# Attention and gated MLP on one core: keys times values of four head pairs as one section, half the keys loaded into U's space, weight sums written to V's space, new orders

## Chip, core and metric

The kernel runs on one core of a Trainium2 chip. The metric is the time of one execution on the device in microseconds (us); less is better. Five engines take part, each with its own instruction queue: TensorE (PE, with its weight loads as PEld), VectorE (DVE), ScalarE (ACT), GpSimd (POOL) and SyncE (SP). In this kernel POOL and SP do little but issue DMAs.

## What is computed

The inputs q, k, v have 8 batches, 8 heads, 576 positions and 64 channels. A linear attention with RMS norm gives x, and a gated MLP with a spatial product follows:

```python
kv = np.einsum('bhsd,bhse->bhde', k, v)
out = np.einsum('bhsd,bhde->bhse', q, kv)
rms = np.sqrt(np.mean(out * out, axis=-1, keepdims=True) + 1e-06)
x = (out / rms * g_norm)          # heads side by side: 8 x 576 x 512
h = np.maximum(x @ w_in, 0.0)     # 512 x 1024
u, v = h[..., :512], h[..., 512:]
v_n = (v - mean(v)) / np.sqrt(var(v) + 1e-06)
v_s = np.einsum('ts,bsd->btd', w_spatial, v_n) + b_spatial[None, :, None]
out = (u * v_s) @ w_out           # 512 x 512
```

All data are float32; w_in and w_out come as 64-bit numbers that the kernel decodes itself.

## The kernel before

**Products.** A large matmul is split: each float32 operand becomes a high and a low part of the type fp32r (`split`, or XH/XL, VH/VL, GH/GL), and three products high*high, high*low, low*high go to one bank (`three`, `hv_k`, `multiply`). For u and for the spatial product, batches 1 to 7 and 2 to 7 use a scheme with seven block products in place of eight (`u_steps`, `sp_steps`; their orders are the tables SEVEN and GATED). It needs sums of blocks: `x_sums` adds blocks of x (batch by batch), `w_sums` adds blocks of w_in once, in batch 1, and writes the sums to a DRAM buffer `spare_u`, from which each batch's `to_u` loads them into UX (L878).

**Attention.** A batch has four pairs of heads. `att_k` takes keys times values of some pairs in float32 on 64x64 quarters of the array (L162, bank `pskv`), the copies L179 and L180 put the result in KVB (even batches) or KVO0/KVO1 (odd ones), `att_q` multiplies it with the queries (L234, bank `pso`) and normalises (L217 to L226), `att_t` transposes (L262, bank `pstr`), and L255/L256 split x into XH and XL. Each batch of 1 to 7 has two sections of two pairs, a section being the matmuls of one call of `att_k`. SP loads keys and values (L142, 512 KB a pair, into the two buffers KV0 and KV1; a remainder of 64 rows into KT0 and KT1 at L143) and queries (L152). A load is issued by `issue`, when fewer than two pairs lie in wait, and waits for the section that last read its buffer.

**MLP.** `hv` forms v (L345, bank `psh`; ReLU L318, norm L324 to L332, split L348/L349), the u steps fill U, the spatial products (banks psa, psb, psc) end in a tail product from TA and TB (L559, L561), `gate` multiplies with U (L573, L575) and splits into G, and `out_unit` multiplies G with w_out (L312, bank `pso2`), copies the bank on ACT to a tile `o` (L655) and stores it (L657). The four banks of the pool ps_mm serve psh, the u products, the spatial products and pso2 in turn. The tile `o` has two buffers of the tag "stg", and so have the tiles `w` into which `w_sums` puts its parts before POOL writes them out (L475): the same two buffers.

**Order.** Batch 0 with all weights' decoding is a prologue set by the table PLAN (letters for steps; W is a weight load, L an attention load). Batch 1 follows FIRST, even batches EVEN, odd ones ODD: v, u, p, o are units of the MLP, s is the next attention step of a later batch, w one half of `w_sums`. The framework's scheduler may move instructions between these marks.

The lines that are needed:

Of the kernel before, what the change touches and what calls it, by code (L numbers as in the profile page):

```python
# [8 lines left out]
F32 = mybir.dt.float32  # L9
# [8 lines left out]
DM, FF = 512, 1024  # L18
# [28 lines left out]
p10 p11 p60 p21 p20 p61 p50 p70 p51 p71 p41 p30 p40 p31  # L47
# [3 lines left out]
p10 p11 p60 p50 p70 p20 p40 p61 p51 p21 p30 p71 p41 p31  # L51
# [3 lines left out]
p p p p s p p p p p p s p p p p o s w s s s o o o s s s s w o s s  # L55
# [3 lines left out]
v s s s v v v u s y s s s s u u u u u s u u u u u s u u u s s s s p p p p p s p s s s p s s p p p p  # L59
s p s s p p o o o o s s s  # L60
# [3 lines left out]
v v v u v u u u u u u s u u s u u u u u s s p p s p p p s p p p s p s p p p s s p p s o s o o s s s  # L64
o s o
# [8 lines left out]
def body(ctx: ExitStack, tc, qT, kvm, kvt, g2, w_in, wsT, bsp, w_out, out):  # L74
# [43 lines left out]
    KVB = persistent([P, 2, P], F32, "KVB")  # L118
    KVO = [persistent([P, 2, P], F32, f"KVO{i}") for i in range(2)]
# [3 lines left out]
    KT = [persistent([P, 2, P], F32, f"KT{i}") for i in range(2)]  # L123
# [12 lines left out]

    def att_load(b, p, kind):
        if kind in "fek":
            kv, kt = (x[n_load[0] % 2] for x in (KV, KT))
            n_load[0] += 1  # L140
            for i, j in ((0, 2), (2, NC)) if (b, p) == (0, 0) else ((0, NC),):
                nc.sync.dma_start(kv[:, :, i:j], kvm[b, p, :, :, i:j])  # L142
            nc.sync.dma_start(kt[0:TAIL], kvt[b, p])  # L143
            keys[b, p] = kv, kt, None
        if kind == "k":
            qs = load.tile([P, P], F32, name="qs", tag="qs")
            nc.sync.dma_start(qs, qT[b, p, :, S - P:S])
            keys[b, p] = kv, kt, qs
        if kind in "fq":
            n = NT if b % 2 else S  # L150
            qt = load.tile([P, S], F32, name="qt", tag="qt")
            nc.sync.dma_start(qt[:, 0:n], qT[b, p, :, 0:n])  # L152
            queries[b, p] = qt

    def att_k(b, pairs, st, copy=nc.vector.tensor_copy):
        ps = ps_att.tile([P, 512], F32, name="pskv", tag="att")
        to = KVO[pairs[0] // 2] if b % 2 else KVB
        ends, first = [], None

        def product(p, of, h, c):  # L160
            at = (p - pairs[0]) * P + h
            return nc.tensor.matmul(ps[h:h + D, at:at + D], of[:, 0, h:h + D], of[:, 1, h:h + D],  # L162
                                    start=c == 0, stop=c == NC)

        for p in reversed(pairs):
            kv, kt, qs = keys.pop((b, p))
            for c in range(NC + 1):
                of = kv[:, :, c] if c < NC else kt
                for h in (0, D):
# [5 lines left out]
            st[p] = to[:, p % 2]  # L175
            ends.append((p, qs))
        both = ps[:, 0:len(pairs) * P].rearrange("p (j e) -> p j e", e=P)
        own = slice(p % 2, p % 2 + len(pairs))
# [107 lines left out]
    def att_steps(b):  # L286
# [12 lines left out]
        K = [lambda p=p: att_k(b, (p, p + 1), st) for p in (0, 2)]  # L299
# [3 lines left out]
        if b % 2 == 0:  # L303
            return [K[0], Q[0], Q[1], T[0], K[1], Q[2], T[1], Q[3], t2, T[3], end], []
# [156 lines left out]
    def w_sums(kk):  # L461
# [315 lines left out]
    for b in range(1, B):  # L777
# [4 lines left out]
        todo += [(b, p, kind) for kind, ps in kinds for p in ps]  # L782
    states = {}
    wanted = [0]

    def issue():

        while wanted[0] and todo and (len(queries) if todo[0][2] == "q" else len(keys)) < 2:
            wanted[0] -= 1
            att_load(*todo.pop(0))  # L790
# [4 lines left out]

    nc.vector.memset(KVB[:, 1], 0.0)
    nc.vector.memset(epsc, EPS)
# [4 lines left out]
    for kvb in KVO:  # L802
        nc.gpsimd.memset(kvb, 0.0)
# [120 lines left out]
    def first():  # L924
# [4 lines left out]
        for d in range(4):  # L929
            if d == 2:  # L930
                enqueue(2)
                enqueue(3)
# [9 lines left out]
    def batch(b):  # L942
# [6 lines left out]
        if b % 2 and b > 1:  # L949
            enqueue(b + 1)  # L950
            enqueue(b + 2)
        for token in (FIRST if b == 1 else ODD if b % 2 else EVEN).split():
# [8 lines left out]
            elif token == "p":  # L961
                p.pop(0)()
            elif token == "o":
# [62 lines left out]
```

## Time and profile before

| | us |
|---|---|
| runs | 507.4, 507.61, 505.15 (median 507.4) |
| profiled execution | 505.66, span 503.9 |
| busy share of PE, DVE, ACT, POOL | 97%, 76%, 58%, 7% |

The profile follows one execution; its span, from the first to the last recorded event, is 1.8 us under that execution's time. A busy share is an average over stages, so the waits of PE (the queries on waits and the timeline) tell more than the shares do.

### The profile page before, as it was taken

How to read it: one execution, taken by the hardware profiler on the slowest of the kernel's cores; microseconds unless marked ns; L12 is line 12 of the kernel's file. 1: busy time of each engine (PE TensorE's matmuls, PEld its weight loads, DVE VectorE, ACT ScalarE, POOL GpSimd, SP SyncE). 2: the span in 40 equal slices, each digit the busy share in tenths (PEclk: the TensorE clock that was granted, in tenths of full speed). 3: DMA queues.
4: the chain of work that ended last, by engine and by line, in shares of the span. 5: the costliest groups of instructions: out<-in, count | busy, mean ns of one | idle time of the engine just before them, and what ended most of it. 6: DMA issues, size and time to landing. Idle time of an engine off the chain costs nothing.

```text
span 503.9 us, 9784 instructions
## 1 busy us (share of the span) xinstructions
PE 487.6 (97%) x3520; PEld 441.4 (88%) x3520; DVE 380.5 (76%) x1016; ACT 291.0 (58%) x1013; POOL 35.6 (7%) x70
## 2 busy tenths in 40 slices
PE   7699999999998999999999999999999999999996
PEld 6579999998987899889998899989998899978995
DVE  1597978866967697967985789868788579986870
ACT  3789854956415894468433686457732587446421
POOL 5000110000002210010000000010000101010000
PEclk8999999999999999999999999999999999999999
DMA  7998352453164648361274426343461514124213
GB/s 233 320 327 265 103 160 74 157 189 126 48 184 132 188 128 291 120 211 42 80 250 131 146 59 231 119 156 119 147 220 44 187 44 153 46 52 157 100 70 105
DMA packets 28917, 74.51 MB, mean 148 GB/s; under 512 B 3810, under 2 KB 8418, under 8 KB 27332
## 3 DMA queue, kind: packets, MB, share of 16 engines
q1 hardware_dynamic: 23412, 48.01, 29.8%
q0 software_dynamic: 5456, 25.87, 15.5%
q8 instruction: 28, 0.46, 0.4%
q14 instruction: 21, 0.17, 0.1%
HBM read 58.48 MB, written 13.11 MB: 142 GB/s over the span
## 4 chain that ended last, share of the span: by engine, by line
PE 56%; issue 19%; ACT 11%; DVE 7%; DMA 4%; POOL 1%; SPq 1%; POOLq 0%; ACTq 0%; DVEq 0%
PE pso L312 13%; PE psh L345 9%; PE psb L553 5%; PE psc L553 4%; PE psa L553 3%; PE psub L553 3%; PE pso L234 3%; ACT x L217 2%; PE psuc L553 2%; PE psua L553 2%; PE pskv L162 2%; PE psu L553 2%; PE pstr L262 2%; PE psh L312 2%; DMA stage<-w_in 1%
## 5 line engine op out<-in xcount | busy, mean ns | idle before, releaser
L312 PE MATMUL pso<-WO,G 128*128 128x512 f32 x384 | 94.1, 396 | 0.0
L312 PEld LDWEIGHTS pso<-WO,G 128*128 128x128 f32 x384 | 70.7, 188 | 14.8 <-ACT o L655 0.4
L348 ACT CAST G<-SUMg 128x288 fp32r<-128x288 f32 (+1 forms) x56 | 22.9, 408 | 51.5 <-DVE SUMg L575 51.0
L217 ACT ACTIVATE x<-pso 128x64 f32<-128x64 f32 x216 | 46.2, 254 | 9.1 <-PE pso L234 9.0
L345 PE MATMUL psh<-WVH,XH 128*128 128x512 f32 x112 | 44.3, 395 | 1.6 <-ACT o L655 1.6
L655 ACT COPY o<-pso 128x512 f32<-128x512 f32 x35 | 19.9, 591 | 44.0 <-PE pso L312 35.4
L217 ACT ACTIVATION_READ_ACCUMULATOR x<-pso 128x1 f32 x216 | 45.2, 238 | 0.0
L345 PE MATMUL psh<-WVH,XL 128*128 128x512 f32 x112 | 43.9, 392 | 0.0
L345 PE MATMUL psh<-WVL,XH 128*128 128x512 f32 x112 | 43.7, 390 | 0.0
L349 DVE TENSOR_TENSOR VL<-v,VH 128x512 fp32r<-128x512 f32 (+1 forms) x56 | 34.4, 621 | 8.5 <-ACT VH L348 8.0
L348 ACT CAST VH<-v 128x512 fp32r<-128x512 f32 (+1 forms) x56 | 31.3, 570 | 5.4 <-DVE v L377 4.1
L349 DVE TENSOR_TENSOR G<-SUMg,G 128x288 fp32r<-128x288 f32 (+1 forms) x56 | 23.4, 419 | 6.0 <-ACT G L348 5.7
L324 DVE BATCH_NORM_STATS2 s<-v 128x6 f32<-128x512 f32 x32 | 22.0, 689 | 7.3 <-ACT v L318 7.1
L345 PEld LDWEIGHTS psh<-WVH,XH 128*128 128x128 f32 x112 | 21.0, 188 | 6.5 <-ACT o L655 2.5
L255 ACT ACTIVATE XH<-pstr,gcol 128x512 fp32r<-128x512 f32 x28 | 19.5, 699 | 12.0 <-PE pstr L262 10.0
L332 ACT ACTIVATE v<-v,mv,rv 128x512 f32<-128x512 f32 x28 | 23.0, 823 | 5.5 <-DVE mv L331 5.5
L553 PE MATMUL psb<-WSH,VH 128*128 128x288 f32 x84 | 25.9, 309 | 0.0
L345 PEld LDWEIGHTS psh<-WVH,XL 128*128 128x128 f32 x112 | 21.0, 188 | 4.4
L553 PE MATMUL psb<-WSL,VH 128*128 128x288 f32 x84 | 24.7, 295 | 0.0
L345 PEld LDWEIGHTS psh<-WVL,XH 128*128 128x128 f32 x112 | 21.0, 188 | 4.2
L553 PE MATMUL psb<-WSH,VL 128*128 128x288 f32 x84 | 24.5, 294 | 0.0
L234 PE MATMUL pso<-KVB,qt 128*128 128x128 f32 x128 | 19.6, 287 | 3.5 <-ACT KVB L180 2.3
(245 smaller groups left out, 1429.0 us busy)
## 6 DMA issues: line engine op xcount, KB each, us to landing
KV<-kvm SPq DMA_DIRECT2D x31, 512.0 KB, 4.9
WO<-spare_o POOLq DMA_DIRECT2D x12, 1024.0 KB, 6.5
UX<-spare_u POOLq DMA_DIRECT2D x18, 512.0 KB, 5.7
out<-o SPq DMA_DIRECT2D x32, 256.0 KB, 2.3
qt<-qT SPq DMA_DIRECT2D x16, 288.0 KB, 4.5
stage<-w_in SPq DMA_DIRECT2D x8, 512.0 KB, 7.0
qt<-qT SPq DMA_DIRECT2D x16, 256.0 KB, 3.2
KT<-kvt SPq DMA_DIRECT2D x32, 64.0 KB, 4.7
```

The costliest lines, as they stand in the source:

```text
L162: return nc.tensor.matmul(ps[h:h + D, at:at + D], of[:, 0, h:h + D], of[:, 1, h:h + D], start=c == 0, stop=c == NC)
L217: nc.scalar.activation(x[:, cols], ps[0:rows, cols], AF.Square, accum_out=ss[:, h:h + 1])
L234: nc.tensor.matmul(ps[:, c * P:(c + 1) * P], qt[:, c * P:(c + 1) * P], st[p], start=True, stop=True)
L255: nc.scalar.activation(hi, ps, AF.Copy, scale=gcol)
L312: nc.tensor.matmul(ps, lt, rh, start=i == 0, stop=i == n - 1)
L324: nc.vector.bn_stats(s6, v)
L332: nc.scalar.activation(v, v, AF.Identity, bias=m, scale=r)
L345: nc.tensor.matmul(ps, lt, rh, start=k == 0 and i == 0, stop=k == NP - 1 and i == 2)
L348: nc.scalar.copy(hi, x)
L349: nc.vector.tensor_tensor(lo, x, f32(hi), op=ALU.subtract)
L553: nc.tensor.matmul(ps, lt, rh, start=start and i == 0, stop=stop and i == len(pairs) - 1, skip_group_check=True)
L655: nc.scalar.copy(o, ps)
```

## The change

Keys times values of batches 3 to 7 become one section of four pairs, the token k; the result goes to one KVB for four pairs, and KVO0 and KVO1 go. Of these batches (and of batch 0) pairs 2 and 3 are loaded into the space of U, which is free between a batch's last gate and the next batch's first u step; the token l issues these loads, two batches ahead of their batch. KT has four tiles. Batch 0's pairs 2 and 3 lie in U, too, with their queries in SUMp1 and SUMu2, so that none of its loads waits for a buffer. The parts in `w_sums` are written to VH and VL in place of the `stg` tiles. All order tables are new.

```diff
+[ W G | L N8 c C J00 D00 L W B00 J01 L c W L A01 n6 C X0 T00 B01 J02 c W W A02 T01 H00 J03 W B02 C
...
-v v v u v u u u u u u s u u s u u u u u s s p p s p p p s p p p s p s p p p s s p p s o s o o s s s
-o s o
+v v v v k u u u u u u u u u u u s u u u s u s p p p s p s p p p p p p p p p s p s o l o o s s o o
...
-    KVB = persistent([P, 2, P], F32, "KVB")
-    KVO = [persistent([P, 2, P], F32, f"KVO{i}") for i in range(2)]
+    KVB = persistent([P, NP, P], F32, "KVB")
...
+    KVU = [flat_u[:, i * n_kv:(i + 1) * n_kv].rearrange("p (j c e) -> p j c e", c=NC, e=P) for i in range(2)]
+    QSU = [flat_u[:, 2 * n_kv + i * P:2 * n_kv + (i + 1) * P] for i in range(2)]
+    def in_u(b, p):
+        return p > 1 and b not in (1, 2)
...
+            if in_u(b, p):
+                kv, kt = KVU[p - 2], KT[p]
+            else:
+                kv, kt = KV[n_load[0] % 2], KT[n_load[0] % 2]
+                n_load[0] += 1
...
+            if kind == "f" and p > 1:
+                qt = SUM[("p1", "u2")[p - 2]].rearrange("p j t -> p (j t)")
...
-        K = [lambda p=p: att_k(b, (p, p + 1), st) for p in (0, 2)]
+        K = [] if b > 2 else [lambda p=p: att_k(b, (p, p + 1), st) for p in (0, 2)]
...
-            parts = [work.tile([P, DM], F32R, name="w", tag="stg", bufs=2) for _ in range(2)]
-            parts = [w.rearrange("p (n f) -> p n f", f=HF)[:, 0:n.stop - n.start] for w in parts]
+            parts = [w[:, kk, n] for w in (VH, VL)]
...
+            elif token == "k":
+                if b + 1 < NB:
+                    att_k(b + 1, range(NP), states.setdefault(b + 1, {}))
+                if b % 2 == 0:
+                    enqueue(b + 1)
+            elif token == "l":
+                if b + 2 < NB:
+                    for p in (2, 3):
+                        att_load(b + 2, p, "k" if b % 2 else "e")
```

The lines move by 9 to 15: L162 becomes L174, L180 L192, L345 L357, L312 L324, L553 L564, L561 L572, L575 L586, L655 L666, L475 L486. PE has the same matmuls in both kernels.

**SP at the start of the program**, before. The names are the loads' targets: gcol the norm's factors, KV and KT keys and values of a pair, qt its queries, stage a block of w_in.

```order
L907 DMA gcol_109<-g2 128x1
L142 DMA KV0_104<-kvm 128x2x256 x2
L143 DMA KT0_106<-kvt 64x256
L152 DMA qt_152<-qT 128x576
L675 DMA stage_176<-w_in 128x1024
L142 DMA KV1_105<-kvm 128x1024
L143 DMA KT1_107<-kvt 64x256
L152 DMA qt_205<-qT 128x576
L142 DMA KV0_104<-kvm 128x1024
```

And now:

```order
L686 DMA stage_149<-w_in 128x1024
L922 DMA gcol_109<-g2 128x1
L151 DMA KV0_102<-kvm 128x2x256 x2
L152 DMA KT0_104<-kvt 64x256
L164 DMA qt_155<-qT 128x576
L151 DMA KV1_103<-kvm 128x1024
L152 DMA KT1_105<-kvt 64x256
L164 DMA qt_206<-qT 128x576
L686 DMA stage_208<-w_in 128x1024
L151 DMA U_100<-kvm 128x1024
L152 DMA KT2_106<-kvt 64x256
```

The first block of w_in goes ahead of all; the second one goes ahead of the third pair's keys, which now go to U.

**PE between batches 2 and 3.** Before, batch 4's first section lies among batch 2's spatial products, and its second one directly behind the last tail product (psc); the output products (pso2) follow:

```order
L553 MATMUL psc_2523<-WSH_84,VL_95 128x288
L559 MATMUL psc_2523<-WTH_86,TA0_96 128x288
L561 MATMUL psc_2523<-WTL0_87,TB0_98 128x288
L262 MATMUL pstr_2999<-ident_108,x_2917 128x128 x4
L162 MATMUL pskv_3022<-KV1_105 64x64 x8
L162 MATMUL pskv_3022<-KT1_107 64x64 x2
L162 MATMUL pskv_3022<-KV0_104 64x64 x8
L162 MATMUL pskv_3022<-KT0_106 64x64 x2
L312 MATMUL pso2_2596<-WO_2313,G_2312 128x512 x8
L312 MATMUL pso2_2612<-WO_2313,G_2312 128x512 x3
```

Now one section of four pairs of batch 4 stands behind batch 2's last output products and ahead of the first product of batch 3 (psh); between the last tail product and the section lie 39 products of pso2, of which these are the last 14:

```order
L324 MATMUL pso2_2618<-WO_2299,G_2298 128x512 x7
L324 MATMUL pso2_2634<-WO_2299,G_2298 128x512 x7
L174 MATMUL pskv_2803<-U_100 64x64 x8
L174 MATMUL pskv_2803<-KT3_107 64x64 x2
L174 MATMUL pskv_2803<-U_100 64x64 x8
L174 MATMUL pskv_2803<-KT2_106 64x64 x2
L174 MATMUL pskv_2803<-KV1_103 64x64 x8
L174 MATMUL pskv_2803<-KT1_105 64x64 x2
L174 MATMUL pskv_2803<-KV0_102 64x64 x8
L174 MATMUL pskv_2803<-KT0_104 64x64 x2
L357 MATMUL psh_2671<-WVH_76,XH_89 128x512
L357 MATMUL psh_2671<-WVL_77,XH_89 128x512
```

The section has pairs 3 and 2 (from U) first. The same place it has at the other boundaries from batch 1 to batch 6; from 1 to 2, 12 output products follow it, and from 3 to 4 and 5 to 6, 43 products lie ahead of it.

**POOL at the sums of w_in.** Before, the parts leave from w tiles, and the last one stands behind the first load of UX:

```order
L475 DMA spare_u_82<-w_1838 128x256
L475 DMA spare_u_82<-w_1839 128x256
L475 DMA spare_u_82<-w_1844 128x2x256
L475 DMA spare_u_82<-w_1845 128x2x256
L475 DMA spare_u_82<-w_1990 128x256
L475 DMA spare_u_82<-w_1991 128x256
L475 DMA spare_u_82<-w_1996 128x2x256
L878 DMA UX_2019<-spare_u_82 128x1024
L475 DMA spare_u_82<-w_1997 128x2x256
L878 DMA UX_2019<-spare_u_82 128x1024 x2
```

Now they leave from VH and VL:

```order
L486 DMA spare_u_82<-VH_94 128x256
L486 DMA spare_u_82<-VL_95 128x256
L486 DMA spare_u_82<-VH_94 128x256
L486 DMA spare_u_82<-VL_95 128x256
L486 DMA spare_u_82<-VH_94 128x2x256 x2
L486 DMA spare_u_82<-VL_95 128x2x256 x2
L893 DMA UX_1939<-spare_u_82 128x1024 x3
L410 DMA TB0_98<-TA0_96 64x768
L410 DMA TB1_99<-TA1_97 64x768
```

All eight DMAs to spare_u stand ahead of the loads of UX (a row with x2 is two).

## Rows read from the trace of the kernel before

**Rows 1.** Part 1 of the page: busy time by engine

```profile
PE 487.6 (97%) x3520; PEld 441.4 (88%) x3520; DVE 380.5 (76%) x1016; ACT 291.0 (58%) x1013; POOL 35.6 (7%) x70
```

**Rows 2.** PE's waits: line, awaited operation, us in total, times, longest

```profile
PE pstr L262 <- DVE x L226: 2.3, 1, 2.3
PE pso L234 <- ACT KVB L180: 2.3, 3, 1.2
PE psh L345 <- ACT o L655: 1.6, 2, 1.4
...
PE psua L553 <- ACT U L506: 0.7, 1, 0.7
```

**Rows 3.** Timeline of PE around a section: start, us, instruction, count

```profile
250.55 0.29 PE L553 MATMUL psb<-WSH,VL 128*128 128x288 f32 x1
250.77 0.69 PE L162 MATMUL pskv<-KV 128*64 128x64 f32 x16
...
252.09 0.40 PE L553 MATMUL psc<-WSH,VL 128*128 128x288 f32 x1
252.33 0.30 PE L559 MATMUL psc<-WTH,TA 128*128 128x288 f32 x1
252.46 0.30 PE L561 MATMUL psc<-WTL,TB 128*128 128x288 f32 x1
```

**Rows 4.** Timeline of PE from batch 1 to 2; in brackets the wait

```profile
152.74 2.00 PE L312 MATMUL pso<-WO,G 128*128 128x512 f32 x8
156.14 0.50 PE L345 MATMUL psh<-WVH,XH 128*128 128x512 f32 x1 [1.40 <-ACT o L655]
156.47 0.39 PE L345 MATMUL psh<-WVL,XH 128*128 128x512 f32 x1
156.70 0.40 PE L345 MATMUL psh<-WVH,XL 128*128 128x512 f32 x1
```

**Rows 5.** Timeline of ACT there

```profile
155.52 0.57 ACT L655 COPY o<-pso 128x512 f32<-128x512 f32 x1
```

**Rows 6.** Timeline of DVE there

```profile
151.18 0.43 DVE L349 TENSOR_TENSOR w<-v,w 128x256 fp32r<-128x256 f32 x1 [4.21 <-DMA out<-o]
```

**Rows 7.** Timeline of POOL, 160 to 176 us: UX's loads

```profile
167.26 0.57 POOL L878 DMA_DIRECT2D UX<-spare_u  x1 [0.95 <-DMA spare_u<-w]
...
173.60 1.12 POOL L878 DMA_DIRECT2D UX<-spare_u  x2 [5.05 <-DMA spare_u<-w]
```

**Rows 8.** Timeline of PE: last tail products of batches 2 and 5

```profile
205.59 0.29 PE L561 MATMUL psc<-WTL,TB 128*128 128x288 f32 x1
...
380.93 0.30 PE L561 MATMUL psc<-WTL,TB 128*128 128x288 f32 x1
```

**Rows 9.** Timeline of DVE: last gates of batches 2 and 5

```profile
210.13 0.46 DVE L575 SCALAR_TENSOR_TENSOR SUMg<-U,SUMg 128x288 f32<-128x288 f32 x1
...
381.75 0.46 DVE L575 SCALAR_TENSOR_TENSOR SUMg<-U,SUMg 128x288 f32<-128x288 f32 x1
```

**Rows 10.** Timeline of SP: two pairs' loads

```profile
206.98 0.33 SPq L142 DMA_DIRECT2D KV<-kvm  x1
...
207.96 0.54 SPq L142 DMA_DIRECT2D KV<-kvm  x1
```

**Rows 11.** Instructions of L142, 194 to 214 us, their landing

```profile
DMA to landing us min/median/max: 3.6/4.3/4.9
```

**Rows 12.** Timeline of PE in the prologue

```profile
8.03 2.05 PE L234 MATMUL pso<-KVB,qt 128*128 128x128 f32 x8 [1.25 <-DMA qt<-qT]
...
15.17 0.63 PE L262 MATMUL pstr<-ident,x 128*128 128x128 f32 x4 [2.29 <-DVE x L226]
```

**Rows 13.** Timeline of ACT in the prologue

```profile
10.14 0.66 ACT L700 ACTIVATE t<-stage 128x512 f32<-128x512 f32 x1 [2.83 <-DMA stage<-w_in]
...
11.55 0.22 ACT L217 ACTIVATE x<-pso 128x64 f32<-128x64 f32 x1
```

**Rows 14.** Windows: stretch, busy by engine, PE's granted clock, DMA share, GB/s

```profile
8.00:12.00 4.00, 3.97 (x22) 3.96 (x22) 0.87 (x2) 1.80 (x7) 0.00 (x0) 0.62 1.01 358
```

More of the change, by code (lines that the diff above doesn't have):

```diff
@@ L117, in body @@
     U = persistent([P, 4, S], F32, "U")
-    KVB = persistent([P, 2, P], F32, "KVB")
-    KVO = [persistent([P, 2, P], F32, f"KVO{i}") for i in range(2)]
+    KVB = persistent([P, NP, P], F32, "KVB")
     KV = [persistent([P, 2, NC, P], F32, f"KV{i}") for i in range(2)]
-    KT = [persistent([P, 2, P], F32, f"KT{i}") for i in range(2)]
+    KT = [persistent([P, 2, P], F32, f"KT{i}") for i in range(4)]
     ident = persistent([P, P], F32, "ident")
@@ L145, in att_load @@
         if kind == "k":
-            qs = load.tile([P, P], F32, name="qs", tag="qs")
+            qs = QSU[p - 2] if in_u(b, p) else load.tile([P, P], F32, name="qs", tag="qs")
             nc.sync.dma_start(qs, qT[b, p, :, S - P:S])
@@ L150, in att_load @@
             n = NT if b % 2 else S
-            qt = load.tile([P, S], F32, name="qt", tag="qt")
+            if kind == "f" and p > 1:
+                qt = SUM[("p1", "u2")[p - 2]].rearrange("p j t -> p (j t)")
+            else:
+                qt = load.tile([P, S], F32, name="qt", tag="qt")
             nc.sync.dma_start(qt[:, 0:n], qT[b, p, :, 0:n])
@@ L156, in att_k @@
         ps = ps_att.tile([P, 512], F32, name="pskv", tag="att")
-        to = KVO[pairs[0] // 2] if b % 2 else KVB
+        to = KVB
         ends, first = [], None
@@ L174, in att_k @@
                             product(p, of, h, c)
-            st[p] = to[:, p % 2]
+            st[p] = to[:, p]
             ends.append((p, qs))
         both = ps[:, 0:len(pairs) * P].rearrange("p (j e) -> p j e", e=P)
-        own = slice(p % 2, p % 2 + len(pairs))
+        own = slice(p, p + len(pairs))
         copy(to[0:D, own, 0:D], both[0:D, :, 0:D])
@@ L303, in att_steps @@
         if b % 2 == 0:
-            return [K[0], Q[0], Q[1], T[0], K[1], Q[2], T[1], Q[3], t2, T[3], end], []
+            return [*K[:1], Q[0], Q[1], T[0], *K[1:], Q[2], T[1], Q[3], t2, T[3], end], []
         return K + [tail, end], [Q[0], Q[1], T[0], Q[2], T[1], Q[3], T[2], T[3], move_tail]
@@ L781, in body, with room @@
             kinds = [(kind, ps) for ps in ((0, 1), (2, 3)) for kind in (keyed, "q")]
-        todo += [(b, p, kind) for kind, ps in kinds for p in ps]
+        todo += [(b, p, kind) for kind, ps in kinds for p in ps if kind == "q" or not in_u(b, p)]
     states = {}
     wanted = [0]
+    def room(b, p, kind):
+        if kind == "q":
+            return sum((x == 0) <= (y < 2) for x, y in queries) < 2
+        return in_u(b, p) or sum(not in_u(*x) for x in keys) < 2
     def issue():
-        while wanted[0] and todo and (len(queries) if todo[0][2] == "q" else len(keys)) < 2:
+        while wanted[0] and todo and room(*todo[0]):
             wanted[0] -= 1
@@ L796, in body @@
     nc.vector.memset(KVB[:, 1], 0.0)
+    nc.gpsimd.memset(KVB[:, 2:4], 0.0)
     nc.vector.memset(epsc, EPS)
@@ L801, in body @@
         nc.gpsimd.memset(kt[TAIL:P], 0.0)
-    for kvb in KVO:
-        nc.gpsimd.memset(kvb, 0.0)
     nc.gpsimd.memset(WT32[TAIL:P], 0.0)
@@ L931, in first @@
                 enqueue(2)
-                enqueue(3)
             for j in range(2):
```

25 lines of the change are left out of this document (12 added, 13 removed).

## The prediction

> **What bounds the kernel now.** I read the busy shares first: PE is busy for 487.6 of 503.9 us, every other engine for far less [rows 1]. So PE's own queue sets the time, and a change is worth what it takes from PE's work or from PE's waits. PE has the same matmuls in both kernels, so two things can move: what a matmul costs by its neighbours, and the waits. Next the list of PE's waits [rows 2]: the four that stand there are the largest but for the prologue's, and none comes back batch by batch. Third, the timeline of PE at three places: a section of keys times values, the boundary from batch 1 to 2, the prologue. The reader should see in them that a wait of PE shows as a bracket, and that a matmul of 512 columns starts 0.23 us after the one before it (156.47 to 156.70, [rows 4]), one of 288 columns 0.13 us (252.33 to 252.46, [rows 3]). What stands above this pace is what the change can take away. The clock was at its full level but for one stretch, 8 to 12 us, with a mean of 0.62 granted [rows 14].
>
> **The change part by part.**
>
> **One section for two.** [Rows 3] has a section of two pairs. From the start of the last product before it to its own start pass 0.22 us, and from the first product behind it to the next 0.24 us, where 0.13 is the pace: 0.09 and 0.11, so a way in and out costs 0.20 us. The change makes one section of two in five batches: 5 x 0.20 = 1.0 us less. In batch 1 one section of two pairs is now two of one pair: 0.2 more. Sum: -0.8 us. (A section of four pairs then takes 2 x 1.32 = 2.6 us, and 2.8 with its ends.)
>
> **The wait for o from batch 1 to 2.** Eight products start one after the other from 152.74; at 0.23 they end at 154.58, but the next, a psh, starts at 156.14 [rows 4]: 1.56 us. It waits for a bank of the pool of four, which ACT's copy to `o` frees at 155.52 to 156.09 [rows 5]. That copy was late since `o` and the parts `w` share two buffers: DVE's first `w` waited 4.21 us for an output store [rows 6]. With `w` in VH and VL the chain goes: -1.56. What is late next there is the section of batch 3, below. The other wait for `o` (1.6 less 1.4, [rows 2]) stands at the start of batch 7; now, at batches 2 to 6, 2.8 us of section lie between the last output product and psh, but 6 to 7 has no section, so I take the 0.2 as gone at a new order, with 0 to -0.4 as its ends. Sum: -1.8.
>
> **The loads of UX.** The last part left POOL behind UX's first load at 167.26; the other two were issued at 173.60 [rows 7]. The u steps that need UX came late, and PE waited 0.7 us for a copy of U in that stretch [rows 2]. Now all eight parts leave ahead of the loads, and with the buffers free they leave some 4 us earlier (the 4.21 us, [rows 6]). I take the 0.7 as gone; bounds 0 (ACT's copy is late for another reason) and -1.2 (with the waits for TB of the same stretch). Sum: -0.7.
>
> **KVB in one copy, more buffers, new orders.** PE waited for KVB three times, 2.3 us in all, the longest 1.2 [rows 2]; two lie in the prologue, and the third, which I put at 0.3 of the other 1.1, in batch 1's stretch. The copies for four pairs have two instructions where there were four, and stand ahead of hv products, which cover them (48 products of 0.23 us, 11 us). I take -0.3 for that wait, and for the other small ones of the list -0.2; ends 0.5 up (new orders make new waits of the same kind) and -0.8. Sum: -0.5.
>
> **The prologue.** The queries of pair 0 landed, and PE began on them at 8.03, after 1.25 us of wait; ACT had nothing to do until w_in's first block landed at 10.14, decoded it, and squared from 11.55 [rows 12, 13]; the transposes, which wait for the norm, began at 15.17 after 2.29 us. All engines' transfers ran without a pause there (DMA share 1.01 at 358 GB/s, [rows 14]), so the sum of bytes ahead of a block sets its landing. Now w_in goes first: pair 0's queries land where w_in landed, about 10.1, 2 us later; eight products of 128 columns end about 11 to 12 (they took 2.05 us at the lower clock), and the squares follow at once, with ACT's decoding done before: at 11 to 12 against 11.55. So the transposes start between 0.6 us earlier and 0.5 later. Behind them the order is better: pairs 2 and 3 wait for no buffer, w_in's second block comes before pair 2. Two waits for KVB (2.0 of the 2.3) may shrink. I take -0.8, between nothing and those 2.0, with +1.5 (below) and -3.5 (both KVB waits gone, and 1.5 of the transposes' 2.29) as ends.
>
> **The loads into U: a new wait.** The two loads of pairs 2 and 3 wait on SP for the last gate of the batch (it reads U); behind them on SP stand that batch's output stores. Before, a buffer of KV was free as soon as its section was over. PE meets the section soon after. The distance: 39 products of pso2 at 0.23 after the last tail product, 8.9 us, at three boundaries (1 to 2, 2 to 3, 4 to 5), 43, 9.8 us, at two. The load: two pairs, the second (needed first) issued 0.98 us after the first [rows 10], with a landing of 3.6 to 4.9 [rows 11]: 0.98 + 4.9 = 5.9 us, and 0.15 for the issue. The gate's lag behind the last tail product is what matters: in batch 2 from 205.88 to 210.59, 4.7 us, in batch 5 from 381.23 to 382.21, 1.0 us [rows 8, 9]. So a wait is lag + 6.05 - 8.9. With 4.7 it is 1.85 us, with 1.0 nothing; at 9.8 it is 0.95 and nothing. At the boundary 1 to 2 DVE has the w sums beside the gates, so I take the long lag, 1.85. At the others I take the middle, 2.85, which gives 0.0; their spread leaves about 0.1 each. Sum: +2.3; ends 0 and 3 x 1.85 + 2 x 0.95 = 7.5.
> The Trainium skill (DMA: Bandwidth & Descriptors, sections Anatomy of one DMA and Where 436 GB/s comes from) has a fixed 2.0 us a DMA and 436 GB/s; an estimate by that page for the two pairs, 1.18 MB, is 4.7 us. [Rows 10, 11] have 5.9; by the page the waits would be 1.2 us shorter each, and the term about +0.7.
> The stores behind them share the DMA engines with these loads, and ACT's third and fourth copies to `o` wait for the first stores. Four banks hold all four units by then, and the section with the first two psh (2.8 + 5.5 us) covers this; if the cover goes, it is a wait of 1 to 2 us a boundary, in the second rival.
>
> **Sum.** -0.8 - 1.8 - 0.7 - 0.5 - 0.8 + 2.3 = -2.3 us against the profiled 505.66: 503.4. The four executions shown (505.15, 505.66, 507.4, 507.61) have a mean of 506.5, 0.8 above the profiled one. 506.5 - 2.3 = **504.2 us**.
>
> **The rivals.**
> **Slower by late loads into U.** Mechanism: the gates' last stores lag by 4.7 us at every boundary, since DVE has norms, splits and gates in one queue. Price 7.5 in place of 2.3: 506.5 - 4.6 + 7.5 = 509.4. It turns the sign at a mean lag of 4.1 us (5 x (lag + 6.05) - 46.3 = 4.6). For it: batch 2's row. Against it: batch 5's, and that the section stands behind the last pso2 products.
> **No gain: the new orders give back elsewhere what they take.** 97% busy leaves no slack where DVE and ACT are near; the waits of [rows 2] were what an order tuned by the scheduler left over, and a new one may leave as many. The prologue's clock is one place: with the fillers now behind pair 1's products PE may stand idle longer and the lower level last for a second stretch as long as the one seen, 4 us at 0.62, 1.5 us. Then -2.3 + 0.8 + 1.5 = 0.0: 506.5.
> **More gain.** No wait for U at all (lag under 2.85 everywhere, also in batch 1), and the prologue at its lower end: -0.8 - 1.8 - 0.7 - 0.5 - 3.5 = -7.3: 499.2.
> **The change does not do what it says** in one point: if the w sums, which now stand behind all p units, keep the gates and x sums of batch 1's end back, the 1.56 us come back as a longer lag at 1 to 2; that is within the forecast's range.
>
> **How the numbers follow.** The forecast, 504.2, has a chance of 0.42 (its own range 502.5 to 505.8, by +/-1.6 for the ends of the small terms); no gain 0.22, slower 0.20, more gain 0.16. The range that holds 8 in 10 reaches into both outer cases, as far as leaves out half of each: 500.0 to 509.2. About 0.5% (2.5 us) is what a measurement of this kernel tells from no change: against the mean of 506.5, faster by over that means under 504.0, against the three runs' median under 504.9. More gain and about two thirds of the forecast lie there: 0.45. Within 0.5% are the rest of the forecast, no gain but for its edges, and a few hundredths of slower: 0.35. Slower by over 0.5% is the rest, 0.20.
>
> **What would show it.** In the new profile: psh at batch 2's start without a wait for `o`; five sections of 2.8 us; the section's first product waiting for KV's DMA at 1 to 2, by about 2 us, and less than 0.5 at the others; UX's three loads issued in one group ahead of hv's end; the first transposes at 14.6 to 15.7. Wrong if: the sum of PE's waits for DMA into U is over 5 us; or the granted clock is at its lower level in a second stretch; or waits for x or U at new places add up to over 2 us.

## The result: 7 us shorter, three times what was forecast

The changed kernel takes 499.25 us (median of four runs, 497.27 to 499.75) against 506.48 before (505.15 to 507.61): a ratio of 0.9851, with an interval of 0.9811 to 0.9891. Forecast were 504.2 us and a range of 500.0 to 509.2; the measured time lies below the range. The profiled execution of the changed kernel took 497.27 us, the shortest of its four; that of the kernel before took 505.66. So the two traces lie 8.4 us apart, the medians 7.2.

The page of the profile after, its busy times (against [rows 1]):

```profile
span 495.5 us, 9784 instructions
PE 485.0 (98%) x3520; PEld 441.4 (89%) x3520; DVE 378.0 (76%) x1011; ACT 291.0 (59%) x1008; POOL 35.7 (7%) x71
```

PE has the same 3520 matmuls. What it lost are waits. Its list of waits, after (line, awaited operation, us in total, times, longest), against [rows 2]:

```profile
PE pso L246 <- ACT KVB L192: 2.0, 3, 0.8
PE pskv L174 <- DMA KV<-kvm: 1.9, 2, 1.6
PE psw L827 <- DVE epsc L814: 1.1, 1, 1.1
PE pso L324 <- ACT XH L267: 0.7, 1, 0.7
PE pso L324 <- DVE G L361: 0.2, 1, 0.2
```

The waits for `o`, for x at the first transposes, for U and for TB are gone, and none for the loads into U has come: the wait for KV is that of the first pair, in the prologue. New is 0.9 us for casts (XH, G) at the end of batch 1's spatial products.

To see where the time went I use one measure for all kernels: the time from each matmul's start to the next one's, less the pace (0.228 us at 512 columns, 0.132 at 288, 0.112 at 128, 0.032 for one of a section), summed over a stage. It counts all that PE lost, waits, ways in and out and a lower clock, and does not mind where a section stands. A stage ends where the next batch's first psh starts. In us:

| stage | before | after |
|---|---|---|
| 0 to 20 us | 9.8 | 9.3 |
| 20 to 35 us | 3.25 | 1.33 |
| 35 to 58 us | 1.27 | 1.12 |
| 58 us to batch 1 | 1.22 | 0.24 |
| batch 1 | 2.49 | 1.98 |
| batch 2 | 2.49 | 0.71 |
| batch 3 | 0.66 | 0.27 |
| batch 4 | 0.77 | 0.74 |
| batch 5 | 1.07 | 0.28 |
| batch 6 | 1.08 | 0.72 |
| batch 7 | 1.10 | 0.16 |
| sum | 25.2 | 16.9 |

The difference is 8.4 us, which is that of the spans (503.9 and 495.5). The first 20 us differ between executions of one and the same order there: of seven kernels that share the new one, the changed kernel among them, four have 9.3 to 9.8 and three 11.1 to 11.2. The three are those in which PE runs at its lower clock for some 4 us longer, as the section on the prologue shows. The other stages mostly repeat within 0.1 us where PE's order in the stage is the same; the largest exception is 0.5 us (from 35 to 58 us, in the kernel with two sections below). So some 3 us are the prologue, 1.8 batch 2, and the rest is spread.

### The profile page after: what moved, and what is told of

It is laid out like the page before. It is cut to its first block, busy times and chain, and to the rows that moved or that the text cites. A ratio compares the mean times of both kernels' runs of the same rounds, so it can differ in the third digit from the quotient of the medians.

```text
span 495.5 us, 9784 instructions
## 1 busy us (share of the span) xinstructions
PE 485.0 (98%) x3520; PEld 441.4 (89%) x3520; DVE 378.0 (76%) x1011; ACT 291.0 (59%) x1008; POOL 35.7 (7%) x71
## 4 chain that ended last, share of the span: by engine, by line
PE 88%; DVE 4%; ACT 3%; issue 0%; DVEq 0%
PE pso L324 20%; PE psh L357 17%; PE psa L564 7%; PE psb L564 7%; PE psub L564 4%; PE psc L564 4%; PE pso L246 4%; PE psua L564 4%; PE pskv L174 4%; PE psuc L564 3%; PE psu L324 3%; PE psh L324 2%; PE pstr L274 2%; PE psu L564 2%; PE pst L202 1%; PE psc L572 1%
## 5 line engine op out<-in xcount | busy, mean ns | idle before, releaser
L324 PE MATMUL pso<-WO,G 128*128 128x512 f32 x384 | 94.4, 394 | 0.9 <-ACT XH L267 0.7
L324 PEld LDWEIGHTS pso<-WO,G 128*128 128x128 f32 x384 | 70.8, 188 | 16.1 <-ACT G L360 0.9
L666 ACT COPY o<-pso 128x512 f32<-128x512 f32 x35 | 19.7, 588 | 58.4 <-PE pso L324 37.7
L357 PE MATMUL psh<-WVH,XH 128*128 128x512 f32 x112 | 44.3, 395 | 0.0
L361 DVE TENSOR_TENSOR VL<-v,VH 128x512 fp32r<-128x512 f32 (+1 forms) x60 | 36.0, 615 | 10.2 <-ACT VH L360 10.1
L357 PE MATMUL psh<-WVL,XH 128*128 128x512 f32 x112 | 43.7, 390 | 0.0
L357 PE MATMUL psh<-WVH,XL 128*128 128x512 f32 x112 | 43.6, 390 | 0.0
L360 ACT CAST VH<-v 128x512 fp32r<-128x512 f32 (+1 forms) x60 | 33.1, 584 | 6.3 <-DVE v L389 4.5
L246 PE MATMUL pso<-KVB,qt 128*128 128x128 f32 x240 | 32.5, 281 | 1.4 <-ACT KVB L192 1.4
L246 PEld LDWEIGHTS pso<-KVB,qt 128*128 128x128 f32 x240 | 30.1, 196 | 1.9 <-ACT KVB L192 1.7
L267 ACT ACTIVATE XH<-pstr,gcol 128x512 fp32r<-128x512 f32 x28 | 19.1, 687 | 15.7 <-PE pstr L274 15.6
L361 DVE TENSOR_TENSOR T<-SUMu,T 128x576 fp32r<-128x576 f32 x12 | 9.1, 755 | 21.7 <-ACT T L360 21.7
L564 PE MATMUL psb<-WSH,VH 128*128 128x288 f32 x84 | 25.3, 302 | 0.0
L357 PEld LDWEIGHTS psh<-WVH,XL 128*128 128x128 f32 x112 | 21.0, 188 | 4.6
L357 PEld LDWEIGHTS psh<-WVH,XH 128*128 128x128 f32 x112 | 21.0, 188 | 4.4
L357 PEld LDWEIGHTS psh<-WVL,XH 128*128 128x128 f32 x112 | 21.0, 188 | 4.3
```

The lines of the kernel that those rows point to most:

```text
L246: nc.tensor.matmul(ps[:, c * P:(c + 1) * P], qt[:, c * P:(c + 1) * P], st[p], start=True, stop=True)
L267: nc.scalar.activation(hi, ps, AF.Copy, scale=gcol)
L324: nc.tensor.matmul(ps, lt, rh, start=i == 0, stop=i == n - 1)
L357: nc.tensor.matmul(ps, lt, rh, start=k == 0 and i == 0, stop=k == NP - 1 and i == 2)
L360: nc.scalar.copy(hi, x)
L361: nc.vector.tensor_tensor(lo, x, f32(hi), op=ALU.subtract)
```

## The sections and the loads into U

The timeline of PE from batch 2 to 3, after:

```profile
207.02 0.62 PE L324 MATMUL pso<-WO,G 128*128 128x512 f32 x2
207.57 0.69 PE L174 MATMUL pskv<-U 128*64 128x64 f32 x16
...
209.84 0.29 PE L174 MATMUL pskv<-KT 128*64 128x64 f32 x4
210.06 0.50 PE L357 MATMUL psh<-WVH,XH 128*128 128x512 f32 x1
210.39 0.40 PE L357 MATMUL psh<-WVL,XH 128*128 128x512 f32 x1
210.63 0.39 PE L357 MATMUL psh<-WVH,XL 128*128 128x512 f32 x1
```

No bracket: the section of four pairs starts with no wait, and so does psh behind it, which is the place where [rows 4] had 1.40 us for `o` (there from batch 1 to 2; at 151.16 now, without a wait). From 207.57 to 210.06 pass 2.49 us. With the ways in (0.10) and out (0.11) it is 2.69, against two times 1.515 before: 0.34 us less for each of five. The forecast counted only the ways, 0.20; the inside of a section, too, costs more than its half share (1.315 us for two pairs, 2.48 for four).

Why is there no wait for U? Last tail product on PE, last gates on DVE, loads on SP, their landing (of the instructions of L151, 199 to 202 us):

```profile
198.41 0.29 PE L572 MATMUL psc<-WTL,TB 128*128 128x288 f32 x1
```

```profile
198.74 0.46 DVE L584 TENSOR_TENSOR SUMg<-psc,SUMu 128x288 f32<-128x288 f32 x1
199.12 0.82 DVE L586 SCALAR_TENSOR_TENSOR SUMg<-U,SUMg 128x288 f32<-128x288 f32 x2
```

```profile
L151 SPq DMA_DIRECT2D U<-kvm x2: 327/662/996, 200.0 to 200.4; - x2
...
DMA to landing us min/median/max: 3.3/4.2/5.0
```

The last gate ends 1.23 us behind the tail product (198.70 to 199.93). The second load, issued at 200.4, lands after 5.0 us, at 205.4: 2.2 us ahead of the section. At the five boundaries the lag is 1.65, 1.23, 2.28, 1.23 and 2.28 us, and the section never waits. The forecast took 4.7 for one and 2.85 for the others, from gates of the kernel before. In [rows 8, 9] batch 2's last gate came 4.7 us behind its tail product; now, behind batches 2 and 4, a result of psb and one of psc are read one after the other and the two last gates follow at once. Behind batches 3 and 5 another read still stands between the two last gates, and the lag is 2.28.

## The prologue

PE, after, from the first section to the transposes of pair 0:

```profile
6.43 0.70 PE L174 MATMUL pskv<-KV 128*64 128x64 f32 x8 [1.58 <-DMA KV<-kvm]
...
8.90 2.08 PE L246 MATMUL pso<-KVB,qt 128*128 128x128 f32 x8 [0.58 <-ACT KVB L192]
...
11.33 1.12 PE L174 MATMUL pskv<-KV 128*64 128x64 f32 x16
...
13.46 1.16 PE L246 MATMUL pso<-KVB,qt 128*128 128x128 f32 x8 [0.79 <-ACT KVB L192]
14.45 0.39 PE L202 MATMUL pst<-KVB,qt 128*128 128x128 f32 x2
14.68 1.50 PE L850 MATMUL psh<-KVB 128*128 128x128 f32 x12
16.02 0.60 PE L274 MATMUL pstr<-ident,x 128*128 128x128 f32 x4
```

Pair 0's products begin at 8.90, not at 10.1 as forecast, and wait for a copy, not for the queries. The transposes of pair 0 begin later than in [rows 12] (16.02 against 15.17), but without a wait: pair 1's section, its products and the fillers stand ahead of them. The forecast asked only when x is there, and not what PE has to do until then. The clock did not make this gain. For the stretch from 8 to 12 us, which had a granted clock of 0.62 in [rows 14], the window now gives 1.00:

```profile
8.00:12.00 4.00, 3.42 (x28) 3.01 (x28) 0.00 (x0) 1.40 (x12) 0.00 (x0) 1.00 1.02 353
```

But the rows above contradict it. The eight products of pair 0 take 2.08 us from 8.90, those of pair 1 1.16 us from 13.46; at the lower clock of [rows 12] the same eight took 2.05. In this trace products of 128 columns start 0.213 us apart from 1.4 to 11 us, and 0.112 us apart behind 13.5; so PE was at the lower level (1.2 GHz) up to some 13 us; the trace's first record of the clock is at 13.1 us, and the window shows 1.00 where there is none. Read the pace of the matmuls beside the granted clock. In three of the seven kernels pair 1's products are slow as well, as in the one with the old order of the gates:

```profile
13.62 2.08 PE L246 MATMUL pso<-KVB,qt 128*128 128x128 f32 x8 [0.79 <-ACT KVB L192]
```

There the trace has the full clock from 17.6 us. Most of the spread of the first 20 us goes with this.

Between 20 and 35 us the gain, 1.9 us, is that of two waits for KVB which the kernel before had there:

```profile
20.01 1.16 PE L234 MATMUL pso<-KVB,qt 128*128 128x128 f32 x8 [0.76 <-ACT KVB L180]
...
24.68 1.16 PE L234 MATMUL pso<-KVB,qt 128*128 128x128 f32 x8 [1.18 <-ACT KVB L180]
```

Both are gone. The three waits for KVB of the list after (2.0 us) are others, before 20 us: at 8.90 and 13.46 above, and at 18.02 for pair 2.

## Experiments

Twelve kernels, each with three or five rounds against the kernel before on the same chip. "Above pace" is the measure of the table. The kernel before had medians of 505.84 to 507.01 us in these sets, so a difference of about 1 us between the medians of two sets says little by itself; the traces have to show where it is.

**The prologue's order alone.** The old table PLAN in the changed kernel, with batch 0's pairs 2 and 3 still in U:

```diff
-[ W G | L N8 c C J00 D00 L W B00 J01 L c W L A01 n6 C X0 T00 B01 J02 c W W A02 T01 H00 J03 W B02 C
+[ G L N8 J00 W c D00 C L L B00 X0 n6 W J01 T00 A01 c W C J02 c H10 H20 W C L A02 H30 c L J03 B01 X1
...
```

> The changed kernel with the table PLAN of before (the prologue's order), but with batch 0's pairs 2 and 3 still in U. Theory A (the prologue's gain of some 3 us is the new order, 1.9 us of it between 20 and 35 us): the time above TensorE's pace at 58 us goes from 11.8 back to 14 us or more, 2 to 3 us longer in all. Rival (it is the freedom of the loads): within 0.7 us of the changed kernel.

502.25 us (501.04 to 502.68), ratio 0.9922 [0.9893, 0.9951]. Above pace 3.26 us from 20 to 35 and 1.24 from 58 us to batch 1: the values of the kernel before, to 0.02 us; to batch 1 it is 15.6 in all, as before, where the changed kernel has 12.0. The timeline has the old wait back:

```profile
15.17 0.63 PE L274 MATMUL pstr<-ident,x 128*128 128x128 f32 x4 [2.70 <-DVE x L238]
```

The loads' freedom without the order is worth nothing; the order is worth 3 us. The other way round:

**The buffers of batch 0.** Changed kernel, batch 0's keys and queries in the old buffers:

```diff
-        return p > 1 and b not in (1, 2)
+        return p > 1 and b > 2
...
-            if kind == "f" and p > 1:
+            if False:
```

> The changed kernel, but batch 0's pairs 2 and 3 lie again in the two buffers KV0 and KV1 and their queries in the pool's two tiles, so that these loads wait for a buffer. Theory A (the buffers made most of the gain of 2.6 us up to 58 us): 1 to 2.5 us longer, all of it before 35 us. Rival (the gain there is the order of the loads and steps): within 0.5 us.

500.46 us (499.51 to 501.73), ratio 0.9885 [0.9863, 0.9907]. Above pace the stage from 20 to 35 us has 1.27, as low as the changed kernel's 1.33; the one from 35 to 58 goes from 1.12 to 2.81. So of the prologue's gain, 1.7 us need the buffers as well, later than theory A had it; neither part has the whole alone.

**The first block of w_in.**

```diff
-[ W G | L N8 c C J00 D00
+[ G | L N8 W c C J00 D00
```

> The changed kernel, but w_in's first block is loaded behind pair 0's keys, as before the change. Theory A (w_in's block ahead of all gives and takes the same): within 0.6 us. Rival (the block first is the gain of the prologue, as ScalarE decodes it while it would wait): 1 to 2.5 us longer.

503.31 us (502.46 to 505.02), ratio 0.9945 [0.9927, 0.9962], 4 us longer. The reason is neither theory's: the decoding kept its place in ScalarE's order, ahead of the copies to KVB, and the copies waited behind it for a block that now came late. ACT's timeline, PE's, and the window from 8 to 12 us:

```profile
10.88 0.66 ACT L711 ACTIVATE t<-stage 128x512 f32<-128x512 f32 x1 [8.64 <-DMA stage<-w_in]
11.58 0.67 ACT L712 ACTIVATE stage<-stage 128x512 uint32<-128x512 uint32 x1
12.15 0.18 ACT L191 COPY KVB<-pskv 64x64 f32<-64x64 f32 x1
```

```profile
12.61 1.65 PE L246 MATMUL pso<-KVB,qt 128*128 128x128 f32 x6 [6.20 <-ACT KVB L192]
```

```profile
8.00:12.00 4.00, 0.00 (x0) 0.00 (x0) 0.42 (x1) 1.08 (x2) 0.00 (x0) 0.50 0.98 355
```

PE waited 6.2 us with nothing to do. The granted clock was 0.50, the lower of the two levels, and stayed there to 20 us; kernels with the changed order have it up to 13 or 18 us without this wait, so only the end of that stretch can be the wait's. A load and the place of what reads it have to move together; how much w_in's block first is worth in itself this run does not tell.

**The copies to KVB in the prologue.**

```diff
-        "J": lambda b, p: att_k(b, (p,), st[b], nc.scalar.copy),
+        "J": lambda b, p: att_k(b, (p,), st[b]),
```

> The changed kernel, but in the prologue's four sections of one pair VectorE copies the upper half of KVB where ScalarE copied both halves one after the other. Theory A (the three waits of 0.9 to 1.1 us between a section's end and the queries' products hold two copies in a row): 0.2 us less at each of them, 0.4 to 0.8 us shorter. Rival (the wait is latency, not the second copy): within 0.3 us.

498.93 us (497.43 to 500.2), ratio 0.9853 [0.9817, 0.9888]: as the changed kernel. The three waits for KVB still sum to 1.9 us where they had 2.0. From a section's last product to the first one on its copy the three have 2.64 us above pace where the changed kernel has 2.80. The rival holds: the second copy is little of this wait.

**The parts of w_sums in the old kernel.** Only their place changes:

```diff
-            parts = [work.tile([P, DM], F32R, name="w", tag="stg", bufs=2) for _ in range(2)]
-            parts = [w.rearrange("p (n f) -> p n f", f=HF)[:, 0:n.stop - n.start] for w in parts]
+            parts = [w[:, kk, n] for w in (VH, VL)]
```

> The kernel before with one part of the change alone: the parts of w_sums go to VH and VL. Theory A (the shared buffers made the wait of 1.56 us at batch 2's start, and the late loads of UX those at 175 to 191 us): 1.5 to 3 us shorter than the kernel before. Rival (without the new orders other waits take their place): within 0.7 us.

506.55 us (505.3 to 511.25), ratio 1.001 [0.9985, 1.0034]: no gain. The wait at batch 2's start went, as theory A had it, and batch 2 went from 2.49 to 0.69 us above pace. But the scheduler moved other steps, and batches 3 and 5 went from 0.66 to 1.79 and from 1.07 to 2.21, in good part since sections there now wait for their loads, as PE's timeline has it:

```profile
255.99 0.42 PE L162 MATMUL pskv<-KV 128*64 128x64 f32 x7 [0.36 <-DMA KV<-kvm]
...
376.01 0.34 PE L162 MATMUL pskv<-KT 128*64 128x64 f32 x4 [0.73 <-DMA KT<-kvt]
```

**The same part undone in the changed kernel**, the three lines the other way round:

> The changed kernel with one thing undone: the parts of w_sums lie again in the two buffers that the output tile o uses. Theory A (the shared buffers made the wait of 1.56 us at batch 2's start): the wait comes back, 1 to 2 us there, and UX is loaded later; 500.3 to 502 us where the changed kernel has 499.25. Rival (the new order alone took the wait away, since the copies to o come earlier): within 0.5 us of the changed kernel.

512.17 us (512.06 to 513.95), ratio 1.0126 [1.0101, 1.0151]: 13 us longer, far more than theory A said. Batch 2 has 14.6 us above pace where the changed kernel has 0.7; batch 1 has 0.7 less, the other batches are as they were, and 1.1 us more pass behind PE's last product. PE's waits:

```profile
PE psuc L564 <- DMA UX<-spare_u: 2.5, 1, 2.5
...
PE psh L357 <- ACT o L666: 1.9, 2, 1.3
PE psa L564 <- ACT VH L360: 1.9, 1, 1.9
PE psa L572 <- DMA TB<-TA: 1.1, 1, 1.1
```

and POOL, here and (second fence) in the changed kernel:

```profile
165.52 0.57 POOL L893 DMA_DIRECT2D UX<-spare_u  x1 [0.74 <-PE pso L246]
166.09 0.72 POOL L486 DMA_DIRECT2D spare_u<-w  x1
172.58 1.12 POOL L893 DMA_DIRECT2D UX<-spare_u  x2 [5.77 <-DMA spare_u<-w]
```

```profile
135.66 0.73 POOL L486 DMA_DIRECT2D spare_u<-VL  x1 [1.20 <-DVE SUMg L584]
151.64 1.72 POOL L893 DMA_DIRECT2D UX<-spare_u  x3 [15.26 <-DMA out<-o]
```

The waits go on behind each other: `o`, then UX's loads, issued at 172.6 and not 151.6, then VH and TB, and the granted clock falls in the stretches with these waits (0.79 from 173 to 180 us, 0.71 from 190 to 200). The waits on this path sum to some 8 us. The rest of the 14 fits the lower clock, by an estimate from the windows: PE is busy for 11.4 us at 0.50 (177 to 180 and 194 to 204 us), which would take about half as long at the full one. So the new orders need the early chain from the weight sums to UX.

**The order of the gates.** The old table GATED in the changed kernel:

```diff
-p10 p11 p60 p50 p70 p20 p21 p40 p61 p30 p51 p71 p41 p31
+p10 p11 p60 p50 p70 p20 p40 p61 p51 p21 p30 p71 p41 p31
```

> The changed kernel with the table GATED of before, all else as it is. Theory A (the lag of the last gate behind the last tail product is set by the order of the last gates): the lag goes from 1.2 to 2.3 us to 3 to 4.5 us in all batches, the loads into U are issued as much later, and PE waits 0 to 1 us at each of five sections: 0.5 to 3 us longer. Rival (the lag came from attention steps in VectorE's queue, which the new tables EVEN and ODD moved): lag and time as in the changed kernel.

500.87 us (499.19 to 501.86), ratio 0.9888 [0.9863, 0.9913]. The lag is 5.9, 4.0, 2.6, 4.1, 2.6, 4.05 and 3.1 us in batches 1 to 7, with the new EVEN and ODD: theory A holds for the lag in the main (two batches lie under its range, one above). But PE waits at no section. From batch 2 to 3, PE's last tail product and the section:

```profile
198.64 0.30 PE L572 MATMUL psc<-WTL,TB 128*128 128x288 f32 x1
...
209.86 0.69 PE L174 MATMUL pskv<-U 128*64 128x64 f32 x16
```

DVE's last gate there, SP's two loads, and the landing of the one issued last (of L151's instructions from 200 to 205 us, the longest is that one):

```profile
202.53 0.46 DVE L586 SCALAR_TENSOR_TENSOR SUMg<-U,SUMg 128x288 f32<-128x288 f32 x1
```

```profile
201.09 2.25 SPq L151 DMA_DIRECT2D U<-kvm  x2
```

```profile
DMA to landing us min/median/max: 3.2/3.6/4.0
```

The first load goes at 201.09, ahead of the last gate (202.99): it did not wait for that gate, but for those of its own part of U (the same at the other four boundaries, where it goes 1.4 to 2.0 us ahead of the second). Only the second one waits for the last gate, starts at 203.0, 1.9 us behind the first, and lands in 4.0 us, at 207.0: 8.0 us behind the tail product's end at 198.94, where the forecast's sum, lag + 6.05, gives 10.1. The 39 products of the forecast's distance, 8.9 us, would have covered these 8.0; here 48 products lie ahead of the section, which starts at 209.86 and leaves 2.9 us. What the run costs lies elsewhere: 0.9 us more above pace in batch 2 and 1.0 in batch 7, neither at a section.

**The new GATED alone, in the kernel before**, the same lines the other way round:

> The kernel before with the new table GATED alone. Theory A (the table sets the lag of the last gate): the lag falls from 1.0 to 4.7 us to 1.2 to 2.5 us; the time moves little, 0 to 1.5 us shorter, since before nothing waits for that gate but the output products and the sums of x. Rival (the lag is set by attention steps): lag as before, time as before.

505.63 us (503.14 to 506.24), ratio 0.9971 [0.9952, 0.999]. The lag is 1.0 to 3.0 us in place of 1.0 to 4.7; batch 7, which has no attention step at all, goes from 4.05 to 1.23, so there the table alone sets it. It is not all of it: batch 4 keeps 3.0 (3.1 before), as sums of x (0.75 us each) and steps of the norm stand among VectorE's last gates there.

**Loads into U twice.** Each pair's load is followed by the same load again:

```diff
-            for i, j in ((0, 2), (2, NC)) if (b, p) == (0, 0) else ((0, NC),):
+            for i, j in ((0, 2), (2, NC)) if (b, p) == (0, 0) else ((0, NC),) * (1 + (b > 0 and in_u(b, p))):
```

> The changed kernel, but each load of a pair into U is made twice, the second after the first has landed, so that pairs 2 and 3 are there some 4 us later. The scheduler knows of it and puts the section behind the first product group of the next batch. Theory A (the scheduler's place for the section follows the load, so the load's time costs nothing): within 0.5 us of the changed kernel, no wait for U. Rival (the forecast's price, a fixed distance of 39 to 43 products): 1.5 to 3 us of wait at each of five sections, 8 to 15 us longer.

522.68 us (520.66 to 526.39), ratio 1.0321 [1.0272, 1.0371]. Both theories fell. No section waits for U, as A said, since the scheduler put them behind the first psh products (12 of them in batches 2, 4 and 6, 24 in 3 and 5); yet 23 us were lost, more than the rival's 15, and most of it in batches 2, 4 and 6 (6.3, 8.6 and 9.0 us above pace). PE's waits:

```profile
PE psua L564 <- ACT U L517: 8.6, 3, 3.3
PE pstt L282 <- DVE x L238: 3.2, 3, 1.6
PE pskv L174 <- DMA KV<-kvm: 2.4, 2, 1.9
PE pst L202 <- ACT KVB L192: 2.1, 2, 1.5
```

In an even batch the section of the next, odd batch is the head of a chain: the copies to KVB, `pst`, the norm of the tail, `pstt`, the tail's rows. The price of a late load is paid there, in front of `pst`, `pstt` and psua, and in the lower clock that goes with these waits (0.50 from 291 to 297 us). Either the section's later place set this chain back, or it was SP's queue, where the second load waits for the first and the output stores wait behind both. The next kernel has PE's order unchanged and the stores on POOL's queue:

```diff
-            nc.sync.dma_start(out[b, c * P:(c + 1) * P, :], o)
+            nc.gpsimd.dma_start(out[b, c * P:(c + 1) * P, :], o)
```

(and the two stores of the remainder alike).

> The kernel with each load into U made twice, and the output stores issued by GpSimd in place of SyncE; TensorE's order is the same as with the stores on SyncE. Theory A (SyncE's queue did the harm: the second load waits there for the first, and the output stores behind it keep ScalarE's copies to o waiting, 20 us in all): that wait falls below 4 us, and most of the 23 us go, to 500 to 506 us. Rival (the later place of the section and its chain did it): above 516 us.

517.28 us (516.63 to 518.4), ratio 1.0218 [1.0191, 1.0246]. Moving the stores gave 5 of the 23 us back; the other 18 stay, in the same places (psua 4.9, pstt 4.7), as the rival had it. That the section's later place is their cause is argued, not shown: in this run, too, the second load holds SP's queue, and no run moved the section alone. Theory A's measure was a bad one: ScalarE's waits for stores sum to 20.0 us with the loads made twice and to 18.4 here, but to 19.8 in the changed kernel, which lost nothing by them.

**One section as two.**

```diff
-                if b + 1 < NB:
-                    att_k(b + 1, range(NP), states.setdefault(b + 1, {}))
+                for ps in ((0, 1), (2, 3)) if b + 1 < NB else ():
+                    att_k(b + 1, ps, states.setdefault(b + 1, {}))
```

> The changed kernel, but the token k takes keys times values as two sections of two pairs, pairs 0 and 1 first. Theory A (a way in and out of a section costs 0.20 us): five more of them, 1.0 us of TensorE's time above its pace, and 1.0 to 1.5 us longer. Rival (the gain of one section lies in its place and in the loads, not in the way in and out): within 0.4 us.

500.67 us (499.9 to 502.94), ratio 0.9886 [0.986, 0.9913], in the range that theory A gave. Behind the first 20 us it has 3.2 us more above pace than the changed kernel. In batches 2, 3 and 5 it is 0.36 more, which is the price of one more section (0.34); in batches 4 and 6 it is 1.3 more, as PE waits there for VectorE's sums in the u steps, which write U, and not for a load (at 297 to 299 and 416 to 418 us, 0.28 and 0.60 us each time); from 35 to 58 us it is 0.5 more, with PE's order unchanged there; in batch 1 it is 1.06 less. There the first section stands among batch 1's spatial products, and the new wait of the changed kernel is gone. That led to the last kernel:

**Two sections in batch 3 alone**, one from batch 4 on:

```diff
-                if b + 1 < NB:
-                    att_k(b + 1, range(NP), states.setdefault(b + 1, {}))
+                for ps in (((0, 1), (2, 3)) if b == 2 else (range(NP),)) if b + 1 < NB else ():
+                    att_k(b + 1, ps, states.setdefault(b + 1, {}))
```

> The changed kernel, but batch 3's keys times values are two sections of two pairs, pairs 0 and 1 (which do not lie in U) first; batches 4 to 7 keep one section. Theory A (two sections there let the first one stand among batch 1's spatial products, where TensorE otherwise waits 1.2 us for casts of G, and cost 0.34 us more): 0.5 to 1.0 us shorter than the changed kernel, near 498.5 us. Rival (that wait went by the other sections' places): within 0.4 us or longer.

497.59 us (496.24 to 498.92), ratio 0.9815 [0.9784, 0.9845]. This interval and the changed kernel's [0.9811, 0.9891] overlap, so the times alone do not prove it better. The trace shows where it is: batch 1 has 0.96 us above pace in place of 1.98, every other stage behind the first 20 us is the same within 0.05, and in place of a wait of 0.65 and one of 0.24 for casts of XH and G (133.05 in the changed kernel) PE has a section to do:

```profile
133.62 0.60 PE L282 MATMUL pstt<-ident,x 128*128 128x128 f32 x4
134.15 0.69 PE L174 MATMUL pskv<-KV 128*64 128x64 f32 x16
...
135.25 0.29 PE L174 MATMUL pskv<-KT 128*64 128x64 f32 x4
135.47 2.38 PE L324 MATMUL pso<-WO,G 128*128 128x512 f32 x9
```

## Why the prediction was wrong, step by step

| term | forecast | measured |
|---|---|---|
| sections | -0.8 | -1.35 (5 x 0.34 less, 0.35 more for two singles) |
| waits for `o` at batch starts | -1.8 | -1.95 (both gone) |
| loads of UX, TB | -0.7 | -1.6 (all three waits from 175 to 191 us gone) |
| KVB, small waits of batches 3 to 7 | -0.5 | some +0.3 (1.8 gone, 2.1 new) |
| prologue | -0.8 | -3.9 (3.6 less to batch 1, in spite of the 0.35 of the two singles; 0.5 of it in the first 20 us, which scatter by more) |
| loads into U | +2.3 | 0 |
| sum | -2.3 | -8.4 (the terms are rounded; -7.2 by the medians) |

**The loads into U** are the step that failed most plainly: 2.3 us of waits were forecast, and none came. It took the lag from rows of the kernel before, though GATED, which sets most of it, is in the diff, and DVE's new order was to be read: in the even batches two gates and nothing else stand behind the last read of psc, so the lag had to be about one read and two gates, 0.46 + 0.82 us. And it let both loads wait for the last gate, while each waits for its own part of U: even with the old GATED and a lag of 4.05 us the second load landed 8.0 us behind the tail product and not 10.1. So its price of a long lag was wrong as well as the lag. The estimate by the Trainium skill (DMA: Bandwidth & Descriptors, section Anatomy of one DMA), whose fit is for DMAs issued by GpSimd, is 4.7 us for both. The 5.4 measured here for loads issued by SyncE (200.0 to 205.4) lie above it, as the rows of before did; with either figure and the new lag there is no wait.

**The prologue** is the step that was mis-sized most, -0.8 for -3.9. Its reasoning on bytes put pair 0's products at 10.1; they came at 8.90. And it kept the transposes' wait as something that could only shift, where the new order puts 4.7 us of other steps of PE (11.33 to 16.02, a wait of 0.79 among them) into it. It also read the clock as full except from 8 to 12 us; sixteen products of 128 columns from 1.06 us took 3.54 us in the kernel before, which is the lower pace as well. The old PLAN in the changed kernel gives the 3.6 us back. The term stood between nothing and the 2.0 us of the two waits for KVB: both went, from 20 to 35 us, and another 1.0 us between 58 us and batch 1, which it had not named, went as well. In the first 20 us three new waits for KVB (2.0) took most of what the transposes' wait (2.29) gave. The lower end, -3.5, was near in size and was held for the less likely one; it had the two waits right and the new ones not at all. The rival "more gain", with a chance of 0.16, had no wait for U and the prologue at that end, and met the time with 499.2 us. That is partly luck: its sum of -7.3 took sections and UX 1.45 us too small and the small waits 0.8 too favourable, and the sum of the measured terms is -8.4.

**Sections, `o`, UX** were right in mechanism. The 0.20 us of a section left out its inside, another 0.15. UX's term took one wait of three, the other two being in its bound.

**What was right for the wrong reason.** "The orders give back elsewhere what they take" did not come true for the whole, but it is what the single parts show: w_sums' new place alone gave nothing, GATED alone 0.3% by the times. That the parts were made for each other is what these runs suggest; the forecast added them one by one on the old order, which cannot show it.

Open is how much of batches 5 and 7's smaller gain (0.8 and 0.9 us) comes from which table; the tables EVEN and ODD cannot be put back alone, since the new tokens stand in them. The tables SEVEN (the order of the u steps) and FIRST changed, too, and no run put either back: a wait in batch 7's u steps (0.46 us above pace) is gone, and SEVEN may have done that.

## What to carry to other kernels

Where a change has new orders, read the awaited engine's new order at each place that a new wait depends on, and what the waiting engine has to do meanwhile; a lag from the old trace is the lag of the old order. Do not add up parts that were ordered together: one of them was worth nothing alone and 13 us when taken out. And when a load is moved, move its readers' place in the in-order queues with it: the block of w_in moved alone cost 4 us. Before a granted clock of 1.00 is believed, compare the pace of equal matmuls in the stretch with a later one.

## What was not expected of the hardware

A section of 64x64 products costs 0.15 us beyond its products inside as well: 1.315 us for 40 recorded matmuls, 2.48 for 80 and 0.73 for 20 (0.58 for each 20 more). The three waits between a section's end and the products on its copy in the prologue (2.80 us above pace) shrink by only 0.16 us when two engines share the two copies. The lower clock of the prologue ends at different times in executions of the same order: the trace has the full level from 12.5 to 13.3 us in four kernels and from 17.2 to 17.6 in three, and the first 20 us cost 1.3 to 1.9 us more in the latter.
